# Two more token pairs by seven block products in a fused clustered-attention and MLP kernel, with the first heads of batch 1 transposed in the opening

## The chip, the cores and the metric

The kernel runs on one core of a Trainium2 chip. The metric is device time in microseconds (us) of one execution; the time of a kernel is the median of its runs. A profiled execution gives a trace: every instruction of every engine and every DMA with its start and end.

The engines of a core are named as in the profile: PE is the matrix engine (PEld its weight loads, which overlap the products), DVE the vector engine, ACT the scalar engine, POOL the general one, and SP issues DMAs only. Each engine works off its own instructions in order. A DMA is issued by an instruction of an engine's queue (SPq, POOLq, ACTq) and lands some time later.

## The reference

The inputs are `q`, `k`, `v` of shape (4, 8, 768, 64) in float32, 16 centroids per head, `w_in` (512 x 2048) and `w_out` (2048 x 512). Each query and each key belongs to the centroid of its head with the largest cosine; a query attends only to keys of the same centroid.

```
q_assign = argmax(q_n @ c_n^T), k_assign = argmax(k_n @ c_n^T)
scores   = where(q_assign == k_assign, q @ k^T / 8, -1e9)
attn     = softmax(scores) @ v                 # per batch and head
x        = attn as 3072 tokens x 512
h        = x @ w_in
out      = (h * sigmoid(h)) @ w_out            # 3072 x 512, float32
```

## The kernel before

**Attention.** A head (of 32: batch 0's are 0 to 7, batch 1's 8 to 15, and so on) goes through these steps. Its raw q and k are loaded in float32 on SP (L119, L121). They are split into a high and a low half in float16: the high one on ACT (L131), POOL (L133) or DVE (L135), the low one on DVE (L140). The split (`hl`) is transposed into the tile `ab`, for batch 0 by PE with an eviction (L163; L172 on ACT, L174 on DVE), for heads 8 to 31 by one DMA transpose on SP (L149, the function `xpose`). Twelve small matmuls against the centroids give the cluster logits (L188, tile `psN`), DVE sums the halves, takes the maximum and compares (L200, L216, L225), and the one-hot codes are put into spare rows of `ab`: for batch 1 by PE (L254), an eviction (L265 on ACT, L267 on DVE) and a DMA on SP (L269); for batches 2 and 3 by POOL, a DMA transpose and a DMA on POOL (L232, L241, L245). With the codes in these rows the product of a query with a key of another cluster comes out so low that its exponential is zero.

Then come 192 *units*: batch, half `c` of the queries (384 of them), two groups of four heads, head, and one of three pieces of 256 keys. A unit is two matmuls (L362, "qk", into one of two buffers `pS`), one exponential on ACT (L367, `exp`, into a tile `P`, of which there are 16 in turn), and later, for two heads together, 36 matmuls of P with v (L379, "pv"). The raw `v` is loaded at L298 and cast on POOL at L303. The result is normed on DVE (L389, L391) and transposed into `xt`, by PE (L401) or DMA (L420).

**MLP.** For each (batch, half), 384 tokens: 16 pieces ("a") of four matmuls `ph = w_in^T x` (L429), a tanh on ACT (L449) and the gate on DVE (L452) into the tile `gt`; then the product with `w_out` for three tiles of 128 tokens. A *plain* tile takes 16 matmuls 128x512 (L469), in four parts of four, and one eviction (L477 ACT, L479 DVE). A *pair* of token tiles is done by seven block products instead of eight, after Strassen and Winograd: seven parts of eight matmuls 128x256 (L551), whose left sides need four sums of gate tiles on DVE (L533, tiles `sg` and in place), whose right sides need differences of blocks of `w_out` (worked out once on DVE in ten small pieces, `tw_piece` L503), and whose results are put together at L557 (ACT), L560 (DVE), L568 (ACT), L571 (DVE), L577 (DVE), and L584 (DVE), or L590, L596, L598 and L599 for the last pair. A pair across the halves ("x") takes the last tile of half 0 and the first of half 1; the gates of the former are kept for that by two DMAs on SP (`keep`, L514), into tiles that reuse the place of `ab` 10 and 11.

Which tiles are plain and which are pairs stands in `kinds` (L957 to L964). Before: batch 0 has three plain tiles in each half; batch 1 one pair and one plain tile in each half; batches 2 and 3 one pair in half 0, and one across the halves and one in half 1. These are 8 pairs and 8 plain tiles.

**What sets the order.** The instructions of each engine stand in the order in which the program issues them. Two things fix that order:

- The opening, up to about 49 us, is a list written by hand, `plan` (L777). A word is one step: `r11` loads head 11's raw data, `w8` loads the first quarter of w_out (`w8` to `w11`; on POOL's queue, L610), `qk25` and `ex25` are a unit's matmuls and its exponential, `a0`, `e0` are pieces of the MLP, `xe1.A` an eviction on ACT. `w10` and `w11` first copy one element of P of units 22 and 23 on POOL (L603), which holds them back until those exponentials are done.
- After it a planner runs while the program is built. It keeps a clock per engine, a list of ready pieces with a due time (`add`, `either`, which chooses ACT or DVE by backlog), and for PE a choice between qk, pv, an MLP piece and a part of a product (`options`, `tensor_piece`) by estimated costs and a few constants (L815 to L821). A head of batches 1 to 3 goes through it as a `chain` (L858): split, transpose, logits, codes. Its starting points are dates in units, worked out from a formula (L924). The estimated costs change only the order; on the chip an instruction starts when its engine and its semaphores allow.

Before, the loads of heads 8 to 11 stand in the opening, and their splits and transposes come from the planner after it.

Of the kernel before, what the change touches and what calls it, by code (L numbers as in the profile page):

```python
# [34 lines left out]
def kernel(  # L35
# [10 lines left out]
    nc = tc.nc  # L46
# [63 lines left out]
    def raw_tag(n):  # L110
        return f"raw{n % 8 if n < EARLY else 5 + n % 3}"

    def load(job, eng=nc.sync):
        n = len(raws)
        raw = mp.tile([128, 12, D], f32, name="raw", tag=raw_tag(n), bufs=1)
        for dst, ap in job.srcs:
            o = raw[:, dst, :]
            if len(ap.shape) == 2:
                eng.dma_start(o.rearrange("p n d -> p (n d)"), ap)  # L119
# [245 lines left out]
    def exp(u):  # L365
        P = mp.tile([128, 2, HALF], f16, name="P", bufs=16)
# [152 lines left out]
    class Pair:  # L519
# [73 lines left out]
        def c21_last(self, part):  # L593
# [5 lines left out]
            nc.sync.dma_start(self.rows()[:, 0, x], self.ot2[:, x])  # L599
# [82 lines left out]
    def first(op, n, eng, banks):  # L682
# [48 lines left out]
        elif op == "w":  # L731
            w_load(n, {10: 22, 11: 23}.get(n))
# [23 lines left out]
        elif op == "xt":  # L756
            xpose(xj)
# [29 lines left out]
        qk23 px3.3 pt1.1 pe1.D ex23 pt2.0 xc1 py3 qk24 pe2.D w7 r9 xe1.A r10 nm3 ex24 qk25 a0.1 pt3.0 w8 qk26 a1.2  # L787
        pe3.D ex25 w9 e0 e1 w10 e6.3 r11 e4.0 ex26 e2.1 e3.2 e5.3 w11 e7.0
# [21 lines left out]
    clock = dict.fromkeys(("PE", "ACT", "DVE", "POOL", "SP"), 0.0)  # L810
    lanes = {e: [] for e in clock}
# [44 lines left out]
    code_at, tensor_todo, after_unit = {}, [], {}  # L856

    def chain(job, b):  # L858
        def split(t):
            if job.name not in loaded:  # L860
                waiting[job.name] = split
                return
            t = max(t, loaded[job.name] + 0.4)
            either(t, 0.5, 0.72, lambda e: hi(job, "act" if e == "A" else None), lambda t: add("DVE", t, 0.9, lambda: lo(job), turned, 1.5), 1.5)

        def turned(t):
            u = last_use.get(place[job.name] - 12, 0)
# [4 lines left out]
            add("SP", t, 1.5, lambda: xpose(job), lambda t: tensor_todo.append((lands(t, 2.45) + (5.0 if b == 3 else 2.2 if b == 2 else 1.8), 0.35, lambda: logits_1(job), sums)), 0.0 if b == 1 else 3.0)  # L872
# [21 lines left out]

        return split
# [4 lines left out]
    loaded, waiting, values_at = {}, {}, {}  # L900
# [4 lines left out]

    def got(job, t):
        loaded[job.name] = lands(t - 0.25, 1.31)
        if job.name in waiting:
            waiting.pop(job.name)(t)

# [5 lines left out]
    def cast(i, t):  # L916
        if i not in values_at:
            waiting[i] = lambda t: cast(i, t)
        else:
            add("POOL", max(t, values_at[i] + 0.4), 0.6, lambda: cast_v(i))  # L920

    for i in range(H, B * H):
        b, h = divmod(i, H)
        p = int((32 + 3.2 * h, 67+5.0*h, 106+5.2*h)[b - 1]) | 1  # L924
        job = jobs[i]
        if i > H + 3:
            date(max(FIRST, p - (8 + min(h, 4) if b == 1 else 16)), lambda t, job=job: add("SP", t, 1.05, lambda: load(job), lambda t: got(job, t), 3.0))
        if i >= H + 2:
            date(p - (6 if b == 1 else 9), lambda t, i=i, b=b: add("POOL", t, 0.6, lambda: load_v(i, nc.gpsimd), lambda t: got_v(i, t)) if b >= 2 else add("SP", t, 0.7, lambda: load_v(i), lambda t: got_v(i, t)))
        date(p - (3 if b == 1 else 6), chain(job, b))  # L930
        date(p, lambda t, i=i: cast(i, t))
# [74 lines left out]
    def new_pair(b, c, kind):  # L1006
        key = b, c, kind
        at.setdefault(key, {})
        t = (1 if b >= 2 else 0) if kind == "p" and c else 0
        if kind == "x":  # L1010
            r2 = (lambda h: cps[b][h]) if b in cps else tokens(b, 0, NM - 1)
            pairs[key] = Pair(kind, b, tokens(b, 1, 0), r2, NM - 1, SG[kind])
# [247 lines left out]
```

## Time and profile before

| what | value |
|---|---|
| runs (3) | 300.66, 302.79, 306.08 us; median 302.79 |
| the profiled execution | 300.67 us, its span 298.9 us |
| granted clock | 1.00 throughout |

How to read it: the span is what the trace covers, from the first instruction to the last; the execution's own time is 1.8 us more. In the windows view a row gives a stretch of the span, its length, the busy time and number of instructions of PE, PEld, DVE, ACT and POOL, PE's granted clock, the busy share of the 16 DMA engines and GB/s. In the groups by line, "busy, mean ns | idle before" tells the time of all instructions of one line and kind, the mean of one, and how long the engine had stood idle ahead of them and for whom. Matmuls are pipelined, so that the mean of one (379 ns for a 128x512 product) is longer than the step from one to the next. In rows of the timeline the first two numbers are the start and the length in us of a run of equal instructions ("x4"), and a number in brackets is the wait ahead of them. In rows of DMA issues the last number is the time from issue to landing; for several kinds it is a median.

### The profile page before, as it was taken

The page shows a single profiled execution, that of the slowest core. Times are in us where ns is not written, and L with a number is a line of the kernel's source. Part 1 is how long each engine was busy: PE and PEld are TensorE (multiplying, and loading weights), DVE is VectorE, ACT ScalarE, POOL GpSimd, SP SyncE. Part 2 cuts the span into 40 slices and gives each one's busy share as a digit, 9 for nine tenths or more (in the row PEclk, how much of TensorE's full clock was granted, in tenths as well). Part 3 has the DMA queues.
Part 4 walks back from the last instruction along what each step waited for, and adds up shares of the span by engine and source line. Part 5 has one row for each costly group of instructions (what it writes and reads, how often), then busy time and mean ns, then how long its engine had stood idle before and what let it go on. Part 6 is the DMA issues. An engine that isn't in the chain of part 4 may idle for free.

```text
span 298.9 us, 8222 instructions
## 1 busy us (share of the span) xinstructions
PE 289.3 (97%) x3281; PEld 204.2 (68%) x3281; DVE 224.0 (75%) x474; ACT 222.3 (74%) x369; POOL 73.3 (25%) x133
## 2 busy tenths in 40 slices
PE   7899989999999999999999999999999999999994
PEld 3786756566676566667766776668667777776784
DVE  5999558787998599997789759896584535568933
ACT  4899879665896689986788769896887769854410
POOL 2894900010140052545424234232000000000000
PEclk9999999999999999999999999999999999999999
DMA  6789999999897688878899989753300021110114
GB/s 207 226 176 207 196 246 220 160 266 270 190 180 192 172 179 205 182 197 185 202 189 230 182 197 228 173 98 74 99 15 16 25 74 27 36 37 0 37 35 140
DMA packets 77364, 44.61 MB, mean 149 GB/s; under 512 B 56304, under 2 KB 73232, under 8 KB 77328
## 3 DMA queue, kind: packets, MB, share of 16 engines
q1 hardware_dynamic: 72240, 35.68, 52.2%
q0 software_dynamic: 4800, 8.13, 14.2%
q8 instruction: 25, 0.41, 0.6%
q10 hardware_dynamic: 288, 0.30, 0.3%
q14 instruction: 11, 0.09, 0.1%
HBM read 27.30 MB, written 6.29 MB: 112 GB/s over the span
## 4 chain that ended last, share of the span: by engine, by line
PE 78%; DMA 11%; ACT 5%; DVE 2%; issue 1%; POOL 1%; SPq 0%; ACTq 0%
PE ph L429 22%; PE pS L362 16%; PE po L551 15%; PE pO L379 10%; PE po L469 8%; DMA wout_s<-in_moe_w_out_dram 7%; ACT P L367 4%; PE psN L188 3%; PE wide L429 3%; DMA ab<-cd 2%; DMA raw<-in_q_dram 1%; PE wide L551 1%; DVE hl L140 1%; POOL hl L133 1%; ACT cd L265 0%
## 5 line engine op out<-in xcount | busy, mean ns | idle before, releaser
L367 ACT ACTIVATE P<-pS 128x768 f16<-128x768 f32 x192 | 155.1, 819 | 36.2 <-PE pS L362 35.7
L362 PE MATMUL pS<-ab 128*128 128x384 f16 x384 | 92.7, 326 | 0.9 <-DMA ab<-cd 0.5
L429 PE MATMUL ph<-xt,win_s 128*128 128x384 f16 x464 | 89.6, 326 | 0.9 <-DVE gt L452 0.8
L452 DVE SCALAR_TENSOR_TENSOR gt<-tn,ph 128x384 f16<-128x384 f32 x116 | 62.2, 550 | 23.2 <-ACT tn L449 22.2
L429 PEld LDWEIGHTS <-win_s 128*128 128x128 f16 x512 | 48.9, 98 | 31.7 <-issue 1.4
L449 ACT ACTIVATE tn<-ph 128x384 f32<-128x384 f32 x116 | 57.5, 502 | 7.6 <-PE ph L429 5.1
L362 PEld LDWEIGHTS <-ab 128*128 128x128 f16 x384 | 34.7, 98 | 20.5 <-issue 1.2
L379 PEld LDWEIGHTS <-P 128*128 128x128 f16 x1152 | 39.9, 97 | 4.4
L379 PE MATMUL pO<-vt,P 128*128 128x65 f16 x1152 | 41.2, 193 | 0.0
L551 PEld LDWEIGHTS <-gt 128*128 128x128 f16 x312 | 29.5, 98 | 6.2 <-DVE gt L533 0.7
L140 DVE SCALAR_TENSOR_TENSOR hl<-raw,hl 128x768 f16<-128x768 f32 (+3 forms) x35 | 32.5, 930 | 1.2 <-ACT hl L131 0.6
L469 PE MATMUL po<-wout_s,gt 128*128 128x512 f16 x128 | 32.8, 379 | 0.2 <-DMA wout_s<-in_moe_w_out_dram 0.2
L303 POOL CAST vt<-vn 128x384 f16<-128x384 f32 x32 | 19.3, 604 | 48.1 <-DMA vn<-in_v_dram 40.3
L551 PE MATMUL po<-wout_s,gt 128*128 128x256 f16 x168 | 21.3, 273 | 0.1
L245 POOL DMA_DIRECT2D ab<-cdt x16 | 8.9, 559 | 50.0 <-PE pS L362 20.4
L188 PEld LDWEIGHTS <-ab 128*128 128x128 f16 x458 | 17.4, 97 | 4.2 <-DVE ab L174 0.3
L469 PEld LDWEIGHTS <-gt 128*128 128x128 f16 x128 | 12.0, 98 | 10.8 <-issue 0.4
L389 DVE RECIPROCAL zr<-pO 128x6 f32<-128x6 f32 x32 | 6.2, 194 | 17.3 <-PE pO L379 17.0
L391 DVE TENSOR_TENSOR xn<-pO,zr 128x384 f16<-128x384 f32 x32 | 17.8, 557 | 1.1
L188 PE MATMUL psN<-stk,ab 128*128 128x32 f16 (+1 forms) x458 | 18.6, 188 | 0.0
L200 DVE TENSOR_REDUCE L<-psN 128x192 f32<-128x384 f32 (+1 forms) x27 | 14.8, 549 | 3.5 <-PE psN L188 3.4
L232 POOL TENSOR_SCALAR od<-od 128x96 f16<-128x96 f16 x16 | 8.8, 548 | 33.1 <-DVE od L225 32.6
(106 smaller groups left out, 276.8 us busy)
## 6 DMA issues: line engine op xcount, KB each, us to landing
raw<-in_k_dram SPq DMA_DIRECT2D x31, 192.0 KB, 4.0
out_dram<-ot SPq DMA_DIRECT2D x23, 256.0 KB, 2.3
raw<-in_q_dram SPq DMA_DIRECT2D x24, 192.0 KB, 3.9
vn<-in_v_dram SPq DMA_DIRECT2D x16, 192.0 KB, 4.4
vn<-in_v_dram POOLq DMA_DIRECT2D x16, 192.0 KB, 4.0
win_s<-in_moe_w_in_dram POOLq DMA_DIRECT2D x8, 256.0 KB, 7.1
wout_s<-in_moe_w_out_dram POOLq DMA_DIRECT2D x4, 512.0 KB, 18.5
raw<-in_q_dram SPq DMA_DIRECT2D x2, 384.0 KB, 4.3
```

The lines of the kernel that those rows point to most:

```text
L140: nc.vector.scalar_tensor_tensor(out=hl[:, s, 1, :], in0=raws[job.name][:, s, :], scalar=QS, in1=hl[:, s, 0, :], op0=ALU.mult, op1=ALU.sub ...
L188: nc.tensor.matmul(L[:, n % g, :, n // g], ab[:, i, :], stk[:, job.groups[i // 3][0], x : x + w], start=(x == 0), stop=(x + w == 2 * HC),)
L303: nc.gpsimd.tensor_copy(vt[:, :, 0:D], vns.pop(i))
L362: nc.tensor.matmul(pS[:, e, 0:HALF], abs_[kj.name][:, kn, :], rhs, start=True, stop=True)
L367: nc.scalar.activation(out=P, in_=pst.pop(u)[:, :, 0:HALF], func=AF.Exp, bias=0.0, scale=ESC)
L379: nc.tensor.matmul(o[:, (2 * t + h) * VW : (2 * t + h + 1) * VW], Ps[i + h, c, j // 2][:, j % 2, ts(t, 128)], vtb[(i + h) % 13][:, j, 0:VW ...
L391: nc.vector.tensor_tensor(out=xn, in0=ov[:, :, 0:D], in1=zr.unsqueeze(2).to_broadcast([128, 2 * NM, D]), op=ALU.mult)
L429: nc.tensor.matmul(ph[:, 0:HALF], win_s[:, r, ts(fb, 128)], xts[b, c][:, r, :], start=(r == 0), stop=(r == NR - 1))
L449: nc.scalar.activation(out=tn, in_=ph[:, 0:HALF], func=AF.Tanh, bias=0.0, scale=1.0)
L452: nc.vector.scalar_tensor_tensor(out=gt[:, fb, :], in0=tn, scalar=1.0, in1=ph[:, 0:HALF], op0=ALU.add, op1=ALU.mult)
L469: nc.tensor.matmul(po, gts[b, c][:, fc, ts(t, 128)], wout_s[:, fc, :], start=(fc == 0), stop=(fc == NFB - 1))
L551: nc.tensor.matmul(o, l[:, f, :], x[:, x0 : x0 + w], start=(f == 0 and k in begins), stop=(f == HK - 1), skip_group_check=True)
```

## The change

- **Pairs.** Batch 0's half 1 takes one pair and one plain tile; batch 1 is done like batches 2 and 3: one pair in half 0, and one across the halves and one in half 1. That makes 10 pairs and 4 plain tiles. The kept gates of batch 1 have tiles of their own, `cp0` and `cp1`.
- **Buffers.** `P` has 12 buffers instead of 16. The raw tiles of heads 16 on use three places instead of the eight that were used up to head 15; batch 1's keep their eight.
- **Opening.** `hi8.A` puts the first half of head 8's split on ACT, `r11 lo8 ht8` brings the load of raw 11 forward and puts the second half of the split and the DMA transpose of head 8 behind it, ahead of unit 25's exponential; `hi9.D lo9 ht9` do the same for head 9 at the end of the list. The planner takes the logits of heads 8 and 9 as possible from 5.0 and 9.5 us after the opening. The two paced quarters of w_out wait for the exponentials of units 24 and 25 instead of 22 and 23.
- **Last store.** The first of the last two stores is issued on ACT's queue instead of SP's.
- **Planner.** Other constants; dates of splits, loads and casts from lists instead of the formula; loads and casts wait in the plan until the tile that they write is free.

```diff
     def raw_tag(n):
-        return f"raw{n % 8 if n < EARLY else 5 + n % 3}"
+        return f"raw{n % 8 if n < 2 * H else 5 + n % 3}"
...
-        P = mp.tile([128, 2, HALF], f16, name="P", bufs=16)
+        P = mp.tile([128, 2, HALF], f16, name="P", bufs=12)
...
-            cps[b] = [mp.tile([128, HK, 128], f16, name="cp", tag=f"ab{10 + m}", bufs=1) for m in range(2)]
+            cps[b] = [mp.tile([128, HK, 128], f16, name="cp", tag=f"ab{10 + m}" if b > 1 else f"cp{m}", bufs=1) for m in range(2)]
...
-            nc.sync.dma_start(self.rows()[:, 0, x], self.ot2[:, x])
+            (nc.sync if part else nc.scalar).dma_start(self.rows()[:, 0, x], self.ot2[:, x])
...
-            w_load(n, {10: 22, 11: 23}.get(n))
+            w_load(n, {10: 24, 11: 25}.get(n))
...
-        qk23 px3.3 pt1.1 pe1.D ex23 pt2.0 xc1 py3 qk24 pe2.D w7 r9 xe1.A r10 nm3 ex24 qk25 a0.1 pt3.0 w8 qk26 a1.2
-        pe3.D ex25 w9 e0 e1 w10 e6.3 r11 e4.0 ex26 e2.1 e3.2 e5.3 w11 e7.0
+        qk23 px3.3 pt1.1 pe1.D ex23 pt2.0 xc1 py3 qk24 pe2.D w7 r9 xe1.A hi8.A r10 nm3 ex24 qk25 a0.1 pt3.0 w8 qk26 a1.2
+        pe3.D r11 lo8 ht8 ex25 w9 e0 e1 w10 e6.3 e4.0 ex26 e2.1 e3.2 e5.3 w11 e7.0
+        hi9.D lo9 ht9
...
-    PACE, LEAST, GAIN = 1.40, 17, .03
-    HOLD = 6
-    MARGIN = 0.3
-    EARLY_T = 72
+    PACE, LEAST, LESS, GAIN = 1.58, 21, 51, 0.075
+    HOLD, ROUND, SIDE, LEAD = -6, 8, 4, 11
+    MARGIN = 0.5
+    EARLY_T = 60
...
-    moves_end = 11
+    moves_end = 13.0
...
+    turned_at = {"h8": 5.0, "h9": 9.5}
+    weights_at = (3.0, 6.0, 9.5, 13.0)
...
+        def turning(t):
+            tensor_todo.append((t, 0.35, lambda: logits_1(job), sums))
...
+        if job.name in turned_at:
+            return lambda t: turning(turned_at[job.name])
         return split
...
+    SPLIT = [27, 27, 31, 40, 43, 46, 52, 55, 64, 70, 73, 78, 84, 87, 94, 100, 104, 116, 125, 126, 131, 132, 139, 142]
+    AHEAD, VALUES, CAST = [16, 10, 12], [1, 10, 7], [13, 2, 7]
...
-        p = int((32 + 3.2 * h, 67+5.0*h, 106+5.2*h)[b - 1]) | 1
+        p = SPLIT[i - H]
...
+    CROSS, PAIRS = (1, 2, 3), ((0, 1), (1, 0), (1, 1), (2, 0), (2, 1), (3, 0), (3, 1))
     for b, c in kinds:
-        if b >= 1:
-            kinds[b, c] = ["p", 2]
-        if b >= 2:
-            kinds[b, c] = ["x", "p"] if c else ["p"]
+        cross = b in CROSS
+        if (b, c) in PAIRS:
+            kinds[b, c] = ["x", "p"] if cross and c else ["p"] if cross else ["p", 2]
+        elif cross:
+            kinds[b, c] = ["x", 1, 2] if c else [0, 1]
...
+    def kept(b, h, t):
+        old, name = (b, 1, "x"), ("lo2", "hi2")[h]
+        at.setdefault(old, {})
+        if b < B - 1:
+            add("SP", t, 0.7, lambda: keep(b, h), lambda t: tell(old, name, lands(t, 1.0) + 1.5))
+        else:
+            tell(old, name, t)
...
-            need = [gate_at.get((b, c, fb)) for fb in range(4 * n, 4 * n + 4)] + ([bank_at] if n == 0 else [])
+            need = [weights_at[n]] + [gate_at.get((b, c, fb)) for fb in range(4 * n, 4 * n + 4)] + ([bank_at] if n == 0 else [])
...
-                mean, least = sum(works[max(x - 1, 0) : 7]) / len(works[max(x - 1, 0) : 7]), LEAST
-                if x < 3:
-                    stock, mean, least = 1.302 * len(qa) + 0.863 * len(qb) + 20.8 * (x - released), 20.8, 12
+                mean, least = sum(works[max(x - 1, 0) : 7]) / len(works[max(x - 1, 0) : 7]), LEAST if x > 2 else LESS
```

More of the change, by code (lines that the diff above doesn't have):

```diff
@@ L810 @@
     clock = dict.fromkeys(("PE", "ACT", "DVE", "POOL", "SP"), 0.0)
+    clock["DVE"] = 2.0
     lanes = {e: [] for e in clock}
@@ L899 @@
             code_at[job.name] = 4.0 if job.name == "x1" else 0.0
-    loaded, waiting, values_at = {}, {}, {}
+    loaded, waiting, values_at, pv_at, after_pv = {}, {}, {}, {}, {}
+    for n in range(4):
+        pv_at[n] = 0.0
     for n in range(8, 12):
@@ L904, with raw_free @@
         values_at[n] = 0.0
+    split_at, after_split = {i: 0.0 for i in range(H + 2)}, {}
+    def raw_free(i, t):
+        old = max((m for m in range(i) if raw_tag(m + 2) == raw_tag(i + 2)), default=0)
+        if old >= H and old not in split_at:
+            after_split[old] = lambda t: raw_free(i, t)
+        else:
+            add("SP", max(t, split_at.get(old, 0.0) + 0.06), 1.05, lambda: load(jobs[i]), lambda t: got(jobs[i], t), 3.0)
     def got(job, t):
@@ L909, in got, with value_free @@
             waiting.pop(job.name)(t)
+    cast_at, after_cast = {i: 0.0 for i in range(H)}, {}
+    def value_free(i, t):
+        if i - 5 not in cast_at:
+            after_cast[i - 5] = lambda t: value_free(i, t)
+            return
+        t = max(t, cast_at[i - 5] + 0.06)
+        if i >= 2 * H:
+            add("POOL", t, 0.6, lambda: load_v(i, nc.gpsimd), lambda t: got_v(i, t))
+        else:
+            add("SP", t, 0.7, lambda: load_v(i), lambda t: got_v(i, t))
     def got_v(i, t):
@@ L1051, in gated @@
                             tell(key, name + x, max(need))
-                    if (b, c) in ((2, 0), (3, 0)):
-                        old = b, 1, "x"
-                        at.setdefault(old, {})
-                        if b == 2:
-                            add("SP", t, 0.7, lambda h=h: keep(b, h), lambda t, name=name: tell(old, name + "2", lands(t, 1.0) + 1.5))
-                        else:
-                            tell(old, name + "2", t)
+                    if c == 0 and b in CROSS:
+                        kept(b, h, t)
         def then(t):
@@ L1068, in then @@
             elif fb == NFB - 1 and kinds[b, c][0] == 0:
[L1069 removed]
+                qb.extend((b, c, t_, n) for t_ in kinds[b, c] for n in range(4))
         return then
```

79 lines of the change are left out of this document (52 added, 27 removed).

## The prediction

> **What bounds the kernel now.** I read the page first (busy shares, clock), then the stretches of the windows view, then what TensorE (PE) waited for, then the chain of waits.
>
> ```profile
> PE 289.3 (97%) x3281; PEld 204.2 (68%) x3281; DVE 224.0 (75%) x474; ACT 222.3 (74%) x369; POOL 73.3 (25%) x133
> PEclk9999999999999999999999999999999999999999
> ```
>
> ```profile
> 50.00:60.00 10.00, 9.75 (x88) 5.80 (x87) 8.02 (x15) 7.21 (x12) 0.31 (x1) 1.00 1.24 175
> 80.00:90.00 10.00, 10.00 (x115) 6.86 (x113) 9.62 (x23) 9.58 (x18) 3.57 (x8) 1.00 0.99 181
> 120.00:130.00 10.00, 10.00 (x108) 6.50 (x106) 9.96 (x20) 9.53 (x18) 4.24 (x8) 1.00 0.81 196
> ```
>
> ```profile
> PE pS L362 <- DMA ab<-cd: 0.5, 1, 0.5
> PE po L469 <- DMA wout_s<-in_moe_w_out_dram: 0.2, 1, 0.2
> ```
>
> ```profile
> 35.93 22.30 DMA wout_s<-in_moe_w_out_dram
> 58.27 1.02 PE po L469 x4
> 59.62 0.86 PE po L469 x4
> 131.66 0.87 PE po L551 x8
> ```
>
> PE is busy 97% at full clock, and its named waits, these two among them, are short: it is the bound, so PE work removed counts in full, and a wait put into PE's in-order queue counts in full too. DVE comes close to filling its time only in places (9.62 and 9.96 of 10). The chain has one piece that is not an engine: the last quarter of w_out, 22.30 us in flight, landing at 58.23 just as PE wants it. The DMA column of the first window stands at 1.24, its engines full.
>
> **The change, part by part.** The sum is made against the profiled execution, 300.67 us (span 298.9, 1.8 around it). The three runs shown have 302.79 as median and 300.66 as lowest, so the profiled one is at their floor.
>
> *Two more pairs.* Four token tiles less by plain products: L469 goes from 128 to 64 matmuls, 0.86 / 4 = 0.215 us each, 13.8 us out. Two pairs more of 7 products of 8 matmuls: L551 gets 112 more at 0.87 / 8 = 0.109, 12.2 us in. PE: -1.6 us. It is sure, since PE is the bound.
>
> What the pairs cost elsewhere:
>
> ```profile
> L533 DVE TENSOR_TENSOR gt<-gt,sg 128x1024 f16<-128x1024 f16 x8 | 5.5, 688 | 3.9 <-PE wide L551 2.1 <-PE po L551 1.7
> L577 DVE TENSOR_TENSOR ot<-po,uu 128x256 f32<-128x256 f32 x8 | 3.4, 425 | 2.7 <-PE po L551 2.7
> L584 DVE TENSOR_TENSOR ot<-po,uu 128x512 f32<-128x512 f32 x7 | 4.8, 688 | 2.5 <-PE po L551 1.6 <-issue 0.9
> L479 DVE COPY ot<-po 128x512 f32<-128x512 f32 x4 | 2.8, 692 | 2.4 <-PE po L469 2.3
> L568 ACT ACTIVATE uu<-po 128x512 f32<-128x512 f32 x7 | 4.2, 599 | 3.1 <-PE po L551 2.9
> L514 SPq DMA_DIRECT2D cp<-gt x2: 628/664/700, 191.9 to 201.1; - x2
> ```
>
> DVE gets per pair four sums (0.69), two 256-wide adds (0.43) and one 512-wide (0.69), 4.3 us, 8.6 for both, and loses two tile copies of 0.69. These 7 us net fall between about 85 and 170 us, where DVE is at 9.6 to 10 of 10 in the windows above. I cost them at nothing, because each sum stands a piece or more of PE work ahead of the product that reads it, and gates have four banks. If that cover is gone, the price is what DVE overruns: some 3.5 us per pair on windows that are 0.04 to 0.4 us short of full, caught up in the emptier ones between, so 1 to 2 us. ACT gets two 512-wide copies (0.6) and two half as wide, and loses two tile copies; at 74% it has room. The two more keep copies for batch 1 (L514) stand 20 and 11 us of PE work ahead of their readers; hidden.
>
> *12 P buffers for 16.* In the listed opening exp 18 now writes a buffer that the twelve L379 matmuls at 30.96 still read; before, it ran ahead of them.
>
> ```profile
> 30.63 0.81 ACT L367 ACTIVATE P<-pS 128x768 f16<-128x768 f32 x1
> ```
>
> ```profile
> 30.96 0.53 PE L379 MATMUL pO<-vt,P 128*128 128x65 f16 x12
> 31.49 0.48 PE L362 MATMUL pS<-ab 128*128 128x384 f16 x2
> ```
>
> ```profile
> 32.38 0.81 ACT L367 ACTIVATE P<-pS 128x768 f16<-128x768 f32 x1 [0.24 <-ACT P L367]
> ...
> 36.42 1.51 ACT L367 ACTIVATE P<-pS 128x768 f16<-128x768 f32 x2 [0.57 <-PE pS L362]
> ```
>
> It can start at about 31.2 instead of 30.63, 0.6 late; the qk at 31.49 waits for it; ACT's idle 0.24 and 0.57 us further on absorb part, but the h8 split (below) takes the second of these, being a pass of 768 like the exp's, 0.8 us. PE arrives 0.4 us late at 48 us: +0.4 (bounds 0, all absorbed, and 0.6). Exp 12 is 0.2 late, inside the 0.5 us wait for a code copy quoted above.
>
> *Heads 8 and 9 in the opening.* Their splits move from DVE at about 46 to 51 us to ACT and DVE at 36 to 45, into two idle stretches of DVE:
>
> ```profile
> 38.98 2.02 DVE L452 SCALAR_TENSOR_TENSOR gt<-tn,ph 128x384 f16<-128x384 f32 x4 [1.28 <-ACT tn L449]
> ...
> 45.02 0.56 DVE L452 SCALAR_TENSOR_TENSOR gt<-tn,ph 128x384 f16<-128x384 f32 x1 [1.42 <-ACT tn L449]
> ```
>
> ```profile
> L140 DVE SCALAR_TENSOR_TENSOR hl<-raw,hl 128x768 f16<-128x768 f32 (+3 forms) x35 | 32.5, 930 | 1.2 <-ACT hl L131 0.6 <-POOL hl L133 0.3
> ```
>
> The first, 1.28 us, holds h8's second pass (0.93); the second, 1.42, holds h9's two (0.93 and about 0.55) but for 0.1. +0. What counts is the DMA: the transpose of h8 is issued at about 39 instead of 48.15, and PE's twelve logits matmuls of h8 (L188) stand in the new order right behind the qk at 48.64, in front of the ph at 48.96; before they stood at about 60.
>
> ```profile
> 48.64 0.49 PE L362 MATMUL pS<-ab 128*128 128x384 f16 x2
> 48.96 0.81 PE L429 MATMUL ph<-xt,win_s 128*128 128x384 f16 x4
> ```
>
> ```profile
> 38.17 0.48 SPq L119 DMA_DIRECT2D raw<-in_k_dram  x1
> ```
>
> ```profile
> raw<-in_k_dram SPq DMA_DIRECT2D x1, 192.0 KB, 10.2
> ```
>
> ```profile
> 48.15 4.20 SPq L149 DMA_TRANSPOSE ab<-hl  x1
> 54.85 0.37 SPq L298 DMA_DIRECT2D vn<-in_v_dram  x1
> 55.32 4.10 SPq L149 DMA_TRANSPOSE ab<-hl  x1
> ```
>
> ```profile
> ab<-hl SPq DMA_TRANSPOSE x1, 11.0
> ```
>
> ```profile
> vn<-in_v_dram SPq DMA_DIRECT2D x1, 192.0 KB, 6.3
> ab<-hl SPq DMA_TRANSPOSE x1, 7.2
> ```
>
> SP's queue still has the load of raw 11 ahead of that transpose: issued 38.17, landed 10.2 us later, at 48.4. SP's transfers land in the order of issue (the vn of 54.85 at 61.2, the transpose behind it at 62.5), so h8's transpose lands after 48.4 wherever it is issued. How long after?
>
> ```profile
> q1 hardware_dynamic: 1282, 0.33, 91.7%
> q0 software_dynamic: 383, 0.37, 37.4%
> ```
>
> ```profile
> q1 hardware_dynamic: 1612, 0.44, 125.8%
> ```
>
> A transpose of 12 blocks of 128 x 128 f16 is 0.39 MB in 1536 packets of 256 B. The first fence is the queues from 52 to 58 us, h8's transpose (q1) beside the end of w_out (q0): 1282 / 6 = 214 packets per us. The second is 60.5 to 62 us, the next transpose with w_out gone: 1612 / 1.5 = 1075 per us. So it lands at the earliest 1.4 us after 48.4, at 49.8 (w_out no hindrance); at the latest 11.0 us after, at 59.4 (the latency of before, whole). I take 11.0 less the 4.20 that SP spent on issuing it, 6.8, hence 55.2: it is the same transfer beside the same w_out, its issue now done in time. The packet rate gives 1536 / 214 = 7.2, nearly the same. PE comes to the logits at 48.96 + 0.4 = 49.4 and stands 5.8 us (bounds 0.3 and 9.9). Behind them in PE's queue waits all else: ph, qk, so exp and gates too. h9's logits stand 4.4 us of PE work later, about 59.9, and its transpose, next in the queue, has until then; +0.
>
> [...]
>
> *w_out.* Its third and fourth parts are paced by exps 24 and 25 instead of 22 and 23, some 2.5 us later; they lie in a queue that lands its parts one after another until 58.23, so 0. PE wants the fourth 1.3 us of work later, and 6 us later still by the wait: the 0.4 us stall before 58.27 goes, -0.4 (if two transposes in front delay w_out by 2 x 1.4 us and h8's costs nothing, it becomes 1 us instead). The raw and v loads of heads 10 to 13 come behind two transpose issues of 4 us on SP; their splits stand 9 to 19 us of PE work behind them. +0.
>
> *Tail.*
>
> ```profile
> 295.38 0.89 SPq L599 DMA_DIRECT2D out_dram<-ot  x2
> ```
>
> The last two stores are issued one behind the other, 0.45 each; one goes to ACT: -0.3 (0 to -0.45).
>
> *New pacing, load dates, casts.* They move pieces among 8000 instructions and remove none. PE's named waits after 60 us are nearly nothing, so there is nothing to win and up to 1 us to lose; 0.
>
> Sum: -1.6 + 0.4 + 5.8 - 0.4 - 0.3 = +3.9, 304.6 on the profiled level. The median of three runs may fall there or 2.1 above; I add half, 1.1: 305.7 us.
>
> **The rivals.**
>
> *The wait is hidden:* h8's transpose goes at the rate of 1075 per us. For it: in its row 4.2 of the 11.0 us were issue, which now lies long before. Against it: 214 per us beside w_out. Wait 0.3: 304.6 - 5.5 = 299.1, plus 1.1: 300.2. [...]
>
> *The full wait, slower:* the transpose is served only as w_out's packets run out, as before, landing 11.0 us after 48.4. Wait 9.9: 308.7, plus 1.1: 309.8. For it: before, 214 packets per us held until w_out's end at 58.2. It counts as slower (over 308.85) from a landing at 58.4 on.
>
> *DVE becomes the bound:* the wait is hidden, but the pair sums overrun DVE between 80 and 130 us, and code copies come late.
>
> ```profile
> ab<-cd SPq DMA_DIRECT2D x10, 48.0 KB, 3.3
> ```
>
> For heads 14 and 15 the first qk stand 4 and 5 us of PE work behind the copy's issue, and a copy lands 3.3 us after it if SP is free. 1.5 us of DVE's overrun and 1 us of a late copy on top of the hidden case: 302.7. Against it: windows of 9.96 passed without a wait of PE.
>
> *The change doesn't do what it says:* the products are fewer by count of the instructions; only the earlier start could fail, which is the forecast.
>
> **How the numbers follow.** Forecast (wait of 3 to 9 us) 0.43, hidden 0.35, full wait 0.12, DVE 0.06, something unnamed that gains 0.04. Two per cent, about what a measurement of this kernel can tell from no change, is 296.7 to 308.85. Slower: 0.12, and 0.06 of the forecast, whose upper end reaches it: 0.18. Faster: 0.04. Same: 0.78. The range takes in the full wait but for its outer tail and the hidden one down to 298.6 (299.1 on the profiled level, less a few tenths if the P buffers are absorbed): 298.6 to 310. The forecast's own is 302.5 to 308.8.
>
> **What would show it.** PE waiting at L188 for the DMA ab<-hl once, near 49 us, for some 6 us; no wait at L469 for w_out; L551 at 560 matmuls and L469 at 64; exp 18 half a us behind its qk; after 60 us PE gaps as small as before. The forecast is wrong if that transpose lands within 2 us of the raw load ahead of it, or if DVE's windows between 80 and 130 us are full and PE waits there for gates.

## The result, and the profile after

The changed kernel takes 315.75 us (median of 4 runs, 314.76 to 316.65), the kernel before 302.43 (4 runs, 300.66 to 306.08): a ratio of 1.046, 95% interval 1.0395 to 1.0525. It is 4.6% slower, outside the range (298.6 to 310). Executions more than 1.5% above the fastest of their kernel are left out of the ratios, and the profiled ones of two experiments (w_out behind the transpose, the first order made anew) are of that kind, so that no times of theirs are compared. The profiled execution took 316.33 us, 15.7 more than that of before, with a span of 313.8. (Up to the plan, a line of the changed kernel has the number of before less one: L187 is the old L188, L361 the old L362, L428 the old L429, L468 the old L469, L550 the old L551.)

The page's busy shares and clock:

```profile
span 313.8 us, 8370 instructions
PE 290.8 (93%) x3329; PEld 210.0 (67%) x3329; DVE 227.7 (73%) x482; ACT 224.3 (71%) x375; POOL 70.0 (22%) x133
PEclk9999999699999999999999799999999999999999
```

PE's busy time is 1.5 us longer than before (289.3) although it has less to do, and PE is idle 313.8 - 290.8 = 23.0 us instead of 9.6. These two, 1.5 and 13.4, are the 14.9 us by which the span grew; the other 0.7 lie outside the span. The clock row has two dents that the kernel before did not have, in the slices from 55 and from 173 us.

What PE waited for (sum, number, longest):

```profile
PE psN L187 <- DMA ab<-hl: 8.5, 1, 8.5
PE pS L361 <- DMA ab<-cdt: 3.5, 1, 3.5
PE wide L550 <- DVE gt L451: 1.4, 1, 1.4
PE psN L187 <- DVE gt L451: 1.2, 1, 1.2
PE pS L361 <- ACT P L366: 1.0, 1, 1.0
PE wide L550 <- ACT tn L448: 0.6, 1, 0.6
```

The first is the wait that the prediction named, at its place: the logits of head 8 behind the qk at 48.26, in the timeline of PE.

```profile
48.26 0.49 PE L361 MATMUL pS<-ab 128*128 128x384 f16 x2
57.29 0.82 PE L187 MATMUL psN<-stk,ab 128*128 128x32 f16 x12 [8.54 <-DMA ab<-hl]
57.92 1.47 PE L428 MATMUL ph<-xt,win_s 128*128 128x384 f16 x4
...
61.30 0.81 PE L428 MATMUL ph<-xt,win_s 128*128 128x384 f16 x4
```

Four matmuls of ph take 1.47 us at 57.92 and 0.81 at 61.30: behind the wait PE runs slowly for a while. The windows say why (the column behind POOL is the granted clock):

```profile
57.00:58.00 1.00, 0.71 (x13) 0.71 (x14) 0.00 (x0) 0.00 (x0) 0.00 (x0) 0.50 1.25 307
58.00:59.00 1.00, 1.00 (x7) 0.49 (x5) 0.56 (x1) 0.00 (x0) 0.00 (x0) 0.50 1.06 309
...
60.00:61.00 1.00, 1.00 (x7) 0.49 (x5) 0.91 (x2) 0.81 (x1) 0.51 (x1) 0.76 1.12 321
61.00:62.00 1.00, 1.00 (x10) 0.68 (x9) 0.50 (x2) 1.00 (x2) 0.00 (x0) 1.00 1.20 269
...
174.00:175.00 1.00, 1.00 (x7) 0.70 (x5) 0.00 (x0) 0.81 (x1) 0.60 (x2) 0.50 1.21 209
```

From 57.3 to about 60.5 us the granted clock is half: 3.2 us that do the work of 1.6. The same follows the wait of 3.5 us at 170 us. Two times 1.6 us more, less the 1.6 that the products were to save, is 1.6, about the 1.5 by which PE is busier. In the experiments below half clock came behind a shorter wait too: with the old opening behind one of 2.74 us, shown here with the clock behind it. It didn't come behind the one of 2.26 us in "12 buffers for P alone": the two matmuls of qk behind that took 0.50 us, where the two behind the wait of 3.5 us took 0.82.

```profile
149.87 0.59 PE L187 MATMUL psN<-stk,ab 128*128 128x32 f16 x12 [2.74 <-DMA ab<-hl]
```

```profile
151.00:153.00 2.00, 2.00 (x10) 1.26 (x9) 1.91 (x5) 0.09 (x1) 1.07 (x2) 0.50 0.98 121
```

Why did the transpose land so late? SP's queue and the DMA issues from it (in the second and third fence the last number is the time from issue to landing):

```profile
37.65 1.08 SPq L118 DMA_DIRECT2D raw<-in_k_dram  x1
38.83 15.47 SPq L148 DMA_TRANSPOSE ab<-hl  x2
54.35 0.78 SPq L118 DMA_DIRECT2D raw<-in_q_dram  x1
```

```profile
wout_s<-in_moe_w_out_dram POOLq DMA_DIRECT2D x1, 512.0 KB, 18.9
raw<-in_k_dram SPq DMA_DIRECT2D x1, 192.0 KB, 9.0
ab<-hl SPq DMA_TRANSPOSE x1, 18.4
```

Raw 11's second load lands at 37.65 + 9.0 = 46.6, the last quarter of w_out (issued on POOL at 38.13) at 57.0, and head 8's transpose, issued at 38.83, at 57.2. SP's 15.47 us are two issues in a row, head 8's (7.11) and head 9's. The packets of the two queues from 47 to 51 us, and from 57 to 58, when w_out is through:

```profile
q0 software_dynamic: 621, 0.61, 91.3%
q1 hardware_dynamic: 620, 0.16, 31.9%
```

```profile
q1 hardware_dynamic: 927, 0.31, 125.4%
```

621 packets of w_out and 620 of the transpose: as many of the one as of the other. As a packet of w_out moves 1 KB and one of the transpose 256 B, the transpose gets a fifth of the bytes, 155 packets per us; with w_out through, SP's queue moves 927, nearly all of them of a transpose (866 are under 512 B). 1536 / 155 = 9.9 us behind 46.6 are 56.5, and w_out's end at 57.0 comes to about the same. The counts are of all 16 DMA engines together; that each DMA engine takes the two queues by turns, as the second experiment's theory has it, is argued from them and not shown.

Equal counts don't explain every rate, though. In the kernel before, from 55 to 58 us, w_out had only 64 packets left in three us, and SP's queue, by its 256 B a packet with transposes alone, still moved only 543, 181 per us:

```profile
q1 hardware_dynamic: 543, 0.14, 119.7%
q0 software_dynamic: 64, 0.06, 12.1%
```

Why it was so slow there is open. In the changed kernel it sped up as w_out ran out (370 packets from 55 to 56 us, 604 from 56 to 57, of the two transposes together).

### The profile page after: what moved, and what is told of

It is laid out like the page before. It is cut to its first block, busy times and chain, and to the rows that moved or that the text cites. A ratio compares the mean times of both kernels' runs of the same rounds, so it can differ in the third digit from the quotient of the medians.

```text
span 313.8 us, 8370 instructions
## 1 busy us (share of the span) xinstructions
PE 290.8 (93%) x3329; PEld 210.0 (67%) x3329; DVE 227.7 (73%) x482; ACT 224.3 (71%) x375; POOL 70.0 (22%) x133
## 4 chain that ended last, share of the span: by engine, by line
PE 84%; DMA 8%; DVE 3%; ACT 3%; issue 1%; DVEq 0%; ACTq 0%
PE ph L428 22%; PE pS L361 20%; PE po L550 18%; PE pO L378 11%; DMA ab<-hl 6%; PE po L468 4%; PE psN L187 4%; PE wide L428 2%; PE wide L550 2%; ACT P L366 1%; DVE hl L139 1%; DVE gt L451 1%; DMA ab<-cdt 1%; DMA raw<-in_k_dram 1%; ACT tn L448 1%
## 5 line engine op out<-in xcount | busy, mean ns | idle before, releaser
L361 PE MATMUL pS<-ab 128*128 128x384 f16 x384 | 94.0, 329 | 4.6 <-DMA ab<-cdt 3.5
L428 PE MATMUL ph<-xt,win_s 128*128 128x384 f16 x460 | 90.1, 329 | 0.8 <-DVE gt L451 0.8
L428 PEld LDWEIGHTS <-win_s 128*128 128x128 f16 x512 | 49.7, 99 | 32.7 <-issue 2.6
L448 ACT ACTIVATE tn<-ph 128x384 f32<-128x384 f32 x115 | 56.8, 501 | 16.1 <-PE ph L428 14.7
L361 PEld LDWEIGHTS <-ab 128*128 128x128 f16 x384 | 34.8, 98 | 21.7 <-DMA ab<-cdt 3.9
L550 PEld LDWEIGHTS <-gt 128*128 128x128 f16 x376 | 36.0, 99 | 9.0 <-issue 1.9
L550 PE MATMUL po<-wout_s,gt 128*128 128x256 f16 x216 | 28.9, 278 | 0.0
L187 PE MATMUL psN<-stk,ab 128*128 128x32 f16 (+1 forms) x458 | 18.9, 190 | 9.7 <-DMA ab<-hl 8.5
L187 PEld LDWEIGHTS <-ab 128*128 128x128 f16 x458 | 17.4, 98 | 14.7 <-DMA ab<-hl 10.9
L302 POOL CAST vt<-vn 128x384 f16<-128x384 f32 x32 | 17.6, 555 | 42.8 <-DMA vn<-in_v_dram 39.7
L231 POOL TENSOR_SCALAR od<-od 128x96 f16<-128x96 f16 x16 | 10.1, 628 | 53.8 <-DVE od L224 50.6
L550 PE MATMUL po<-tw,sg 128*128 128x256 f16 x144 | 18.3, 273 | 0.0
L550 PEld LDWEIGHTS <-sg 128*128 128x128 f16 x160 | 15.4, 98 | 3.4 <-issue 0.8
L468 PE MATMUL po<-wout_s,gt 128*128 128x512 f16 x64 | 16.4, 379 | 0.0
```

Of the source, the lines that this page charges most:

```text
L187: nc.tensor.matmul(L[:, n % g, :, n // g], ab[:, i, :], stk[:, job.groups[i // 3][0], x : x + w], start=(x == 0), stop=(x + w == 2 * HC),)
L302: nc.gpsimd.tensor_copy(vt[:, :, 0:D], vns.pop(i))
L361: nc.tensor.matmul(pS[:, e, 0:HALF], abs_[kj.name][:, kn, :], rhs, start=True, stop=True)
L428: nc.tensor.matmul(ph[:, 0:HALF], win_s[:, r, ts(fb, 128)], xts[b, c][:, r, :], start=(r == 0), stop=(r == NR - 1))
L448: nc.scalar.activation(out=tn, in_=ph[:, 0:HALF], func=AF.Tanh, bias=0.0, scale=1.0)
L468: nc.tensor.matmul(po, gts[b, c][:, fc, ts(t, 128)], wout_s[:, fc, :], start=(fc == 0), stop=(fc == NFB - 1))
```

## The experiments

Each run is compared with runs of the kernel before on the same chip. These had medians of 301.24 us (13 runs) beside the opening, the buffers and the pairs alone and the first order made anew, 301.3 (19) beside the other two orders made anew and the kernel with fewer stores, and 300.9 (7) beside the rest. Some expectations name the planner's own estimate: that is its clock for PE at the end of the plan, which starts at about 43 us of the trace (252.1 in the kernel before, where PE's last matmul ends at 294.8).

**The wait alone, taken away.** The logits of heads 8 and 9 read a tile that has long been there; every engine's order stays. 

```diff
-        ab = abs_[job.name]
+        other = job.name in ("h8", "h9"); ab = abs_["k7" if other else job.name]
...
-                    L[:, n % g, :, n // g], ab[:, i, :], stk[...],
+                    L[:, n % g, :, n // g], ab[:, i % 6 if other else i, :], stk[...],
```

> The changed kernel with the logits of heads 8 and 9 read from head 7's transposed tile, so that these matmuls wait for no DMA; every engine's order is that of the changed kernel, and heads 8 and 9 get the wrong clusters. Theory A (PE loses the 8.5 us of the wait and about 1.4 us more at the half clock that follows it, and nothing else hangs on that wait): the wait at L187 near 48 us is gone, the granted clock stays at 1.00 there, 316.3 - 8.5 - 1.4 = 306.4 us, with the later waits (1.3 us at 98, 3.7 at 169, 2.3 near 290 us) still there. Rival B (the wait only moves: the first qk of batch 1, or the splits of heads 10 to 13, whose loads SP issued late, are late next): 312 us or more, with a new wait of several us between 60 and 75 us.

306.57 us (304.76 to 313.06, 4 runs; ratio 1.0153, 1.0073 to 1.0232). The window of the wait, and what PE waited for from 40 us on:

```profile
48.00:57.00 9.00, 9.00 (x137) 6.51 (x136) 8.20 (x19) 7.67 (x14) 0.00 (x0) 1.00 1.30 165
```

```profile
PE ph L428 <- DVE gt L451: 2.6, 3, 1.0
PE pS L361 <- DMA ab<-cdt: 1.6, 1, 1.6
PE wide L550 <- DVE gt L451: 1.4, 1, 1.4
PE wide L550 <- ACT tn L448: 0.6, 1, 0.6
```

Theory A holds, 306.57 for 306.4: PE is busy through the whole window at full clock, and no wait took the place of the one removed. Taking the wait away is worth 9.2 of the 13.3 us by the medians; the trace of the changed kernel has 8.5 of wait and 1.6 of half clock for it. What is left after 60 us is 1.8 us for gates (2.6 less 0.8 in the opening, which the kernel before has as well), 1.6 for codes, 2.0 in the last blocks.

**w_out behind the transpose.** The third and fourth quarters wait on POOL for head 8's landing instead of exponentials 24 and 25, and stand at the end of the list.

```diff
-            nc.gpsimd.tensor_copy(pace, Ps[units[after]][0:1, 0, 0:1])
+            nc.gpsimd.tensor_copy(pace, abs_[after][0:1, 0, 0:1])
...
-            w_load(n, {10: 24, 11: 25}.get(n))
+            w_load(n, {10: "h8", 11: "h8"}.get(n))
...
-        pe3.D r11 lo8 ht8 ex25 w9 e0 e1 w10 e6.3 e4.0 ex26 e2.1 e3.2 e5.3 w11 e7.0
-        hi9.D lo9 ht9
+        pe3.D r11 lo8 ht8 ex25 w9 e0 e1 e6.3 e4.0 ex26 e2.1 e3.2 e5.3 e7.0
+        hi9.D lo9 ht9 w10 w11
```

> The changed kernel with the third and fourth quarters of w_out held back on POOL until head 8's transpose has landed; all else as it was. Theory A (while w_out's packets are queued, a DMA engine serves one packet of each queue by turns, 150 to 155 a us of each; the transpose's packets are small and many, 1536, so it crawls until w_out is through): the transpose's packets go on by turns until the second quarter has landed at about 49.6 us, and at over 800 a us from then on; it lands at about 51 us instead of 57.2, PE waits about 2 us instead of 8.5, and the clock stays full; the fourth quarter lands at about 61 and may cost up to 2 us at L468: 308 to 310 us. Rival C (the transpose is slow by itself, or by its place in SP's queue behind raw 11, whatever POOL moves): it lands at about 57 us as before and the time stays at 315 to 317 us, or more.

307.46 us (305.14 to 310.14; ratio 1.0176, 1.0092 to 1.0261). Head 8's wait, and the queues from 52 to 54 us:

```profile
54.78 0.82 PE L187 MATMUL psN<-stk,ab 128*128 128x32 f16 x12 [4.56 <-DMA ab<-hl]
```

```profile
q1 hardware_dynamic: 1028, 0.26, 174.0%
q8 instruction: 1, 0.02, 3.7%
```

The wait is 4.6 us instead of 8.5, so the transpose depends on what POOL moves, and rival C falls. It isn't the 2 us expected: w_out's second quarter was through only at 52 us, and in the two us after it the transpose got 1028 packets where the changed kernel moved 927 in one; a 16 KB packet of instructions was fetched then (that the fetch held it up is not shown). The time is a little below the 308 to 310 expected, which is in part luck: the wait was 2.6 us longer than expected and half clock followed it (0.50 from 54 to 58 us), while the 2 us allowed for w_out's last quarter did not come.

**The opening alone**, in the kernel before: `hi8.A`, `r11 lo8 ht8`, `hi9.D lo9 ht9` and the two dates; pairs, constants and buffers of before.

```diff
+    turned_at = {"h8": 5.0, "h9": 9.5}
...
-        pe3.D ex25 w9 e0 e1 w10 e6.3 r11 e4.0 ex26 e2.1 e3.2 e5.3 w11 e7.0
+        pe3.D r11 lo8 ht8 ex25 w9 e0 e1 w10 e6.3 e4.0 ex26 e2.1 e3.2 e5.3 w11 e7.0
+        hi9.D lo9 ht9
```

> The kernel before with only the opening's edits: heads 8 and 9 split and transposed in the listed part, their logits at 5.0 and 9.5 us of the plan, the last quarters of w_out paced as before; pairs, constants, dates and buffers as before. Theory A (the transposes take turns with w_out's packets and land as w_out ends, whatever the pairs do): one wait of 8 to 10 us at L187/L188 near 49 us, then 2 to 3 us at half clock; 300.9 + 9 + 1.4 less the 1.1 us by which the plan is shorter, 310 us. Rival E (the wait needs the changed kernel's other edits, its later pacing of w_out above all): 301 to 305 us.

312.44 us (311.56 to 313.12; ratio 1.0403, 1.0303 to 1.0502). The wait is there without the pairs and with the old pacing of w_out:

```profile
57.73 0.82 PE L188 MATMUL psN<-stk,ab 128*128 128x32 f16 x12 [8.60 <-DMA ab<-hl]
```

A holds, rival E falls; the 2 us above the expectation are in part a second wait of 1.0 us for a transpose (9.6 us in all for `ab<-hl`).

**12 buffers for P alone**, in the kernel before, with its order:

```diff
-        P = mp.tile([128, 2, HALF], f16, name="P", bufs=16)
+        P = mp.tile([128, 2, HALF], f16, name="P", bufs=12)
```

> The kernel before with 12 buffers for P instead of 16 and nothing else; every engine's order is that of the kernel before. By the prediction's term: exp 18 waits about 1 us for the products at 30 us, PE gets 0.4 us later, 301.3 where the kernel before gives 300.9. By the trace of the changed kernel: PE stands 1.1 us at its second qk after that instead of 0.2, but two waits of the opening near it (0.7 us and 0.4 us in the trace of before) shrink, so the end moves by -0.2 to +0.9 us.

301.09 us (10 runs; ratio 1.0039, 0.9991 to 1.0087): no difference that can be measured. Its profiled execution has a wait that shows something else:

```profile
169.49 0.50 PE L362 MATMUL pS<-ab 128*128 128x384 f16 x2 [2.26 <-DMA ab<-cdt]
```

That is a code landing late in the very order of the kernel before, whose own trace has no such wait there. So codes at 160 to 170 us seem to be on the edge in that order too; how often one slips, a single trace can't tell.

**The pairs alone**, in the kernel before, with its opening, constants and dates (12 P buffers and `cp0`, `cp1` with them):

```diff
-        if b >= 1:
-            kinds[b, c] = ["p", 2]
-        if b >= 2:
-            kinds[b, c] = ["x", "p"] if c else ["p"]
+    CROSS, PAIRS = (1, 2, 3), ((0, 1), (1, 0), (1, 1), (2, 0), (2, 1), (3, 0), (3, 1))
...
```

> The kernel before with only the pairs: 10 pairs and 4 plain tiles, 12 buffers for P and tiles of their own for batch 1's kept gates; opening, constants and dates as before. The planner's own estimate for PE is 5.4 us longer than for the kernel before, with waits of 7.7 us in all that it foresees, most of them at 56 to 67 us of its clock (99 to 110 us of the trace), so I expect 300.9 + 5.4 = 306 us, where PE's work alone would give 299.3. Theory A' (the pairs leave too little work between two units where batch 0's second half and batch 1 meet, unless the order is made anew) holds if the waits come there; rival F (the planner's estimate is wrong, and the products' 1.6 us are gained) gives 299 to 300.

310.49 us (308.92 to 312.43; ratio 1.0333, 1.0236 to 1.0431). Waits from 40 us on:

```profile
PE pS L362 <- DMA ab<-cdt: 3.4, 1, 3.4
PE pS L362 <- ACT P L367: 3.0, 9, 0.6
PE ph L429 <- DVE gt L452: 1.4, 2, 0.8
```

Rival F falls. Theory A' is borne out in part: the qk wait for exponentials nine times, but of the 7.7 us that the planner foresaw, most of them there, only 2.3 (1.7 for exponentials, in six waits, and 0.6 for a gate) lie between 98 and 115 us. The largest single loss was not foreseen: a code that landed 3.4 us late at 164 us, with 3.4 us of half clock behind it, some 5 us in all and about what the expectation is short by. With the constants of before the products' gain is not to be had.

**Logits late, nothing else; and the old opening.** First the changed kernel with later dates, then with the plan's words and the pacing of before.

```diff
-    turned_at = {"h8": 5.0, "h9": 9.5}
+    turned_at = {"h8": 15.0, "h9": 18.0}
```

```diff
-    turned_at = {"h8": 5.0, "h9": 9.5}
+    turned_at = {}
...
-        pe3.D r11 lo8 ht8 ex25 w9 e0 e1 w10 e6.3 e4.0 ex26 e2.1 e3.2 e5.3 w11 e7.0
-        hi9.D lo9 ht9
+        pe3.D ex25 w9 e0 e1 w10 e6.3 r11 e4.0 ex26 e2.1 e3.2 e5.3 w11 e7.0
```

> The changed kernel with the planner told that heads 8 and 9 are transposed 15 and 18 us after the opening instead of 5.0 and 9.5, so that their logits stand behind some 10 us of other work on PE; the transposes are issued where they were. Theory A: no wait at L187 near 48 us, 304 to 308 us, the spread for what the planner makes of the later waits. Rival B (what is held up by the transposes on SP's queue is late anyway): 312 us or more.

> The changed kernel with the opening of the kernel before: heads 8 and 9 are split and transposed by the planner after the listed part, and w_out is paced as before; pairs, buffers and constants stay. Theory A (the opening's early transposes are the loss, the rest is worth its 1.6 us less a few tenths): 300 to 305 us. Rival D (the later waits at 98, 169 and 290 us belong to the pairs and the new constants, and come back here): 305 to 308 us with such waits of 5 to 7 us in all after 60 us.

313.27 us (312.63 to 316.47; ratio 1.0418, 1.0324 to 1.0512) and 313.97 (312.14 to 317.79; ratio 1.0398, 1.0322 to 1.0474). Both speak against A as these expectations put it. The waits of the first, from 46 us on:

```profile
PE pS L361 <- DMA ab<-cdt: 3.4, 2, 3.0
PE pS L361 <- ACT P L366: 2.4, 5, 0.7
PE psN L187 <- DMA ab<-hl: 2.1, 3, 0.8
PE wide L428 <- DVE gt L451: 1.2, 1, 1.2
```

The wait at 48 us is gone, and some 10 us of small ones came. They come with the new order: every date that the planner gets changes its choices from there on, and the constants fit only the dates that they were chosen for. By the planner's own clock PE's work ends at 248.8 us in the changed kernel, at 252.4 with the late logits and at 257.8 with the old opening (252.1 in the kernel before); foreseen waits of over 0.3 us come to 3.6 us in the one and 8.5 in the other, and to 0.4 in the changed kernel. So these two don't part A and B; the first experiment does, as it keeps the order.

**The order made anew.** The late dates as they are on the chip, and constants and split dates chosen so that the planner's clock comes out short: once with its landings (248.8 us), once with every landing 1.0 us later (249.9), and once with the old opening and landings 0.6 later (252.9). The first takes PACE 1.32, LEAST 18, LESS 58, GAIN 0.085, HOLD -15, ROUND 6, SIDE 2 and EARLY_T 47, the third PACE 1.56, LEAST 19, LESS 106, GAIN 0.085, HOLD -22, ROUND 7, LEAD 10, MARGIN 0 and EARLY_T 50, each with split dates of its own. The second:

```diff
-    PACE, LEAST, LESS, GAIN = 1.58, 21, 51, 0.075
-    HOLD, ROUND, SIDE, LEAD = -6, 8, 4, 11
-    MARGIN = 0.5
-    EARLY_T = 60
+    PACE, LEAST, LESS, GAIN = 1.58, 20, 58, 0.065
+    HOLD, ROUND, SIDE, LEAD = -22, 8, 4, 11
+    MARGIN = 0.1
+    EARLY_T = 55
...
-        return moves_end + 1.0
+        return moves_end + 2.0
...
-    turned_at = {"h8": 5.0, "h9": 9.5}
+    turned_at = {'h8': 15.0, 'h9': 16.5}
...
-    SPLIT = [27, 27, 31, 40, 43, 46, 52, 55, 64, 70, 73, 78, 84, 87, 94, 100, 104, 116, 125, 126, 131, 132, 139, 142]
+    SPLIT = [28, 30, 32, 40, 42, 45, 51, 55, 64, 70, 70, 78, 84, 86, 94, 100, 107, 115, 125, 128, 131, 133, 138, 141]
```

> The changed kernel with the planner told that heads 8 and 9 are transposed at 15.0 and 16.5 us (as the trace shows), and its constants and the dates of the splits chosen anew so that its own estimate for PE (248.8 us) is as short as that of the changed kernel, with one foreseen wait of 0.4 us. Theory A (the loss is the wait near 48 us and its half clock, 10.2 us of 13.3; the rest are late codes and the last blocks): no wait there, 306 us if the later waits come back with their 4 to 7 us, 300 if not. Rival B (whatever is not late there is late elsewhere): 312 us as with the later logits alone.

> The changed kernel with the planner told that heads 8 and 9 are transposed at 15.0 and 16.5 us and that every transfer lands 1.0 us later than it assumed, constants and dates of the splits chosen anew under that; its own estimate for PE is 249.9 us where the kernel before has 252.1. Theory A (the loss is the wait near 48 us; what comes late after it are transfers for which the plan leaves too little time): 300.9 - 2.3 = 298.6 us plus 1 to 4 us of late transfers, 300 to 303 us. Rival B (the pairs cannot be placed without 5 us of waits): 305 us or more.

> The changed kernel's pairs with the opening of the kernel before, constants and dates of the splits chosen anew for that; its own estimate for PE is 252.9 us, 0.7 more than that of the kernel before and 4.9 less than that of the old opening with the changed kernel's constants. Theory A (the old opening came out at 314 us because its order had waits that the planner foresaw, not because the pairs are dear): 300.9 + 0.7 = 301.6 us plus 0 to 3 us of late transfers, 302 to 305 us. Rival B (the pairs are dear by themselves): 308 us or more.

The first gave 302.6, 308.19, 309.32 and 310.98 us in four runs, too far apart for a verdict; its profiled execution waits 6.0 us for codes and 2.3 for a transpose. The third gave 307.99 us (ratio 1.0222, 1.0156 to 1.0287), outside A's 302 to 305 and at the edge of B's 308 or more; of its waits 1.5 us are for exponentials, 1.1 for a transposed `xt` and 1.9 lie in the last blocks. By itself it would speak for B. The second gave 299.82 us (10 runs, 298.17 to 305.97; ratio 0.9955, 0.9911 to 0.9998), a little under A's 300 to 303, and with the same pairs it rules B out: it is faster than the changed kernel by 5%, and than the one before by half a per cent, an interval that ends only just below 1. Its page, and its waits from 40 us on:

```profile
PE 287.5 (97%) x3329; PEld 208.4 (70%) x3329; DVE 227.0 (77%) x479; ACT 225.5 (76%) x378; POOL 70.1 (24%) x133
```

```profile
PE ph L428 <- DVE gt L451: 0.8, 1, 0.8
PE psN L187 <- DMA ab<-hl: 0.2, 1, 0.2
PE wide L428 <- DVE gt L451: 0.2, 1, 0.2
```

```profile
ab<-hl SPq DMA_TRANSPOSE x1, 18.2
```

```profile
59.08 0.51 PE L187 MATMUL psN<-stk,ab 128*128 128x32 f16 x12
```

PE is busy 1.8 us less than before (289.3), near the products' 1.6, and about as idle as before (296.6 - 287.5 = 9.1 us, before 9.6). Head 8's transpose takes as long as ever, issued at 39.02 and landed at 57.2; its logits stand at 59.08 and wait for nothing. As constants and split dates changed together with the assumed landings, and one of three such orders came out well, the experiment shows that the pairs have an order without the waits; it doesn't part what each setting gave.

**Fewer stores.** The kernel of the first experiment without the output stores of batches 0 to 2 (18 issues on SP), order unchanged.

```diff
-            nc.sync.dma_start(self.rows()[:, 1:3, :], self.ot.rearrange("p (a e) -> p a e", a=2))
+            self.b < B - 1 or nc.sync.dma_start(self.rows()[:, 1:3, :], self.ot.rearrange("p (a e) -> p a e", a=2))
...
```

> The kernel with the logits of heads 8 and 9 read elsewhere (306.6 us), and with the stores of the outputs of batches 0 to 2 left out: 18 issues of 0.4 to 0.5 us less on SP, 4.7 MB less to move; the order of all else is the same. Theory G (what waits after 60 us, but for the last blocks, are raw loads and codes that land late because SP's queue and the DMA engines are full): the waits at 80 to 84 us (2.1 us) and at 161 us (1.7 us) fall below 0.5 us each, 303 us. Rival H (these waits lie in the order of DVE and POOL): they stay, 306 to 307 us. Both expect the waits of the last blocks (0.7 and 1.5 us) to stay.

302.32 us (10 runs; ratio 1.003, 0.9987 to 1.0074), against 306.57 with the stores (ratio 1.0153). The waits from 40 us on:

```profile
PE ph L428 <- DVE gt L451: 1.6, 3, 0.8
PE wide L550 <- DVE gt L451: 1.4, 1, 1.4
PE psN L187 <- DMA ab<-hl: 1.0, 1, 1.0
PE wide L550 <- ACT tn L448: 0.6, 1, 0.6
```

The wait for codes is gone, that for gates is 0.8 (1.6 less the opening's; below 0.5 was expected) instead of 1.8, one of 1.0 for a transpose came. G holds in the main: with less on SP's queue and the DMA engines the transfers came in time. Which of the two, the run doesn't part.

## Why the prediction was wrong, point by point

- **The steps that failed** are two. By the traces the change costs 15.7 us where the sum had 3.9, 11.8 more. The wait's term was 2.7 too small and its half clock, 1.6, was not in it. *"New pacing, load dates, casts"*, put at 0, lost about 8.3. With the wait and its clock right, the forecast would have been 305.7 + 4.3 = 310.0, the upper end of the range; the larger miss is the term at nothing. The other terms come to less than 1 us together.
- **The wait** failed at "I take 11.0 less the 4.20 that SP spent on issuing it, 6.8, hence 55.2". The transpose landed at 57.2 and PE waited 8.5 us instead of 5.8. "The same transfer beside the same w_out" did not hold. The 214 packets per us were taken from 52 to 58 us of the kernel before, where w_out had become thin: its queue has 383 packets in these 6 us, 64 per us, and 155 when both queues are full. At that rate the transpose gets 155, and it landed just behind w_out's end at 57.0. The issue itself took 7.1 us instead of 4.2. The rival of the full wait put it as "served only as w_out's packets run out", with a landing at 59.4 and 9.9 us of wait; that is what happened, and the wait was 8.5 because the landing came 2.2 us earlier than that (w_out ended 1.2 us earlier than before) and PE 0.7 us sooner than forecast (48.75 for 49.4). (The forecast's own range, 302.5 to 308.8 for waits of 3 to 9 us, should read 302.9 to 308.9.)
- **What the wait costs** was taken as its length. It costs 1.6 us more for the half clock behind it; the trace of before, whose longest wait of PE is 1.2 us, with the clock at 1.00 throughout, could not show that.
- **"Pacing, load dates, casts ... 0"** rested on PE's waits after 60 us being "nearly nothing" in the kernel before, and was bounded at 1 us of loss. But the new constants, dates and pairs make another order, whose waits the old trace can't show: 3.5 us for a late code with 1.6 of half clock behind it, 1.2 us for DVE, 2.0 us in the last blocks. The last is the same in the first, second and last experiment and gone with the order made anew, so it belongs to that order; what in it is at fault was not looked into. The late codes look like a matter of small margins, which is argued and not shown: the same kind of wait came up in one execution of the order of before, and went when stores were left out. Why codes come late there stays open.
- **Products, -1.6:** the counts are 568 and 64 matmuls (456 + 112; the 560 of the prediction left out that the last pair has 8 more, of half width). The size fits roughly: PE is busy 1.8 us less in the order made anew, but that time differs by about 1 us between traces of the same work (289.3 and 290.2 with 16 and 12 buffers, 288.8 and 287.6 in the first and the last experiment). "It is sure, since PE is the bound" left out that the order must still give PE enough to do and the codes time to land: the pairs alone cost 9 us.
- **P buffers, +0.4:** exponential 18 waits about 1 us at the place named, but the end doesn't move (1.0039, 0.9991 to 1.0087).
- **h9's logits +0, w_out -0.4, tail -0.3:** right in kind. There is one wait for a transpose and none for w_out; from the last matmul's end to the span's it is 3.3 us instead of 4.1.
- **DVE as the bound:** it isn't. Between 80 and 130 us the window with most of it has 9.47 of 10 busy, and PE waited once there, 1.2 us.

```profile
90.00:100.00 10.00, 8.83 (x97) 5.76 (x96) 9.47 (x21) 8.31 (x15) 2.02 (x4) 1.00 1.18 182
```

## What to carry to other kernels

Here a transpose of 1536 packets of 256 B, issued at 38.83 us on the DMA engines that were loading w_out in packets of 1 KB, landed at 57.2, just behind the end of w_out at 57.0: put the reader of such a transfer behind the large one's end. Take such a rate from a stretch where both queues are full (155 packets per us here, not 214). In the in-order queue of the bounding engine the waits of 8.5 and of 3.5 us cost 1.6 us each more than their length here. And a new order is a cost of its own, which waits of the old trace don't bound: with new constants and dates, chosen with 1 us more on each landing and the true date of two transposes, the same pairs went from 315.75 to 299.82 us.

## What the runs showed of the hardware

- Half clock for 3.2 us of work behind waits of 8.5 and of 3.5 us (the changed kernel), for 3.4 us behind one of 3.4 (the pairs alone) and at least from 151 to 153 us behind one of 2.74 that ended at 149.87 (the old opening); none behind one of 2.26 us (12 buffers for P alone). In the third order made anew, where no wait of PE from 40 us on was longer than 1.2 us, the clock still averaged 0.994 over the span of 306.3 us, by an estimate from these two numbers 3.7 us at half; so it isn't one long wait alone that brings it.
- Two queues with work on the same DMA engines moved as many packets each, 621 and 620 in 4 us, with packets of 1 KB and of 256 B.
- SP stood 15.5 us in issuing two DMA transposes while w_out was loading (one in the kernel before took 4.20); the loads behind them were issued at 54.35.
